# Nine result buffers, stores behind the last load, and the order around them, in a fused recurrence and mixer kernel

## The chip, the cores and the metric

The kernel runs on one core of one Trainium2 chip. The metric is the device time of one execution in microseconds (us). Six engines' queues matter: TensorE (PE, with its weight loads as PEld), VectorE (DVE), ScalarE (ACT), GpSimd (POOL), and SyncE (SP), which issues most DMAs.

## The reference

There are 4 batches of 768 tokens and 8 heads of 40 features. A recurrence with a 40 x 40 state for each batch and head gives `y`; its heads are joined to `x` with 320 features per token, and a mixer follows: a rotation by learned angles, a mix over all 768 tokens of a batch, and a channel product with a residual.

```python
for t in range(S):
    y[:, :, t] = np.einsum('bhd,bhde->bhe', rt, state)
    Sa = np.einsum('bhde,bhe->bhd', state, at)
    state_decay = state * wt[:, :, None, :] - np.einsum('bhd,bhe->bhde', Sa, bt)
    state = state_decay + np.einsum('bhd,bhe->bhde', vt, kt)
...
theta = x @ w_theta
zr, zi = x * np.cos(theta), x * np.sin(theta)
yr = np.einsum('ts,bsd->btd', w_tok_r, zr)
yi = np.einsum('ts,bsd->btd', w_tok_i, zi)
u = x + yr + yi
return u + np.maximum(u @ w_ch, 0.0)
```

Inputs and the result are fp32.

## The kernel before

**Tiles.** The 3072 tokens are cut into 24 tiles of 128 tokens, numbered 0 to 23; tiles 0 to 5 are batch 0, and so on. The recurrence is done chunk by chunk: within a tile by matrix products with triangular masks, from tile to tile by a state (`gt`).

**Operations.** The function builds a list of 1602 operations. An operation has an engine, a kind and a tile, and the text names it by the two: `y20` is the readout of tile 20. A tile goes through these steps:

| kind | engine | what it does | line |
|---|---|---|---|
| `lw lk lb la lv`, `loadr` | SP | loads of the inputs, 160 KB each; `loadr` is issued twice for two tiles | L409, L421 |
| `ln exp ew wi cs cx` | ACT, DVE, PE | decays: logarithm, running sums, exponentials | L445 to L487 |
| `kb ah v r` | POOL mostly | products with the decays, casts to bf16 | L428 to L435 |
| `tkb ta tv tr tb nut xt ut` | PE, or SP | transposes; `ekb` and the like take them out of PSUM (ACT or DVE) | L391, L538, L711; SP: L698 |
| `spsi sphi slv slu` | PE | four sets of scores, 8 matmuls on half the rows each; `mpsi` and the like mask them (DVE; or ACT and then `sel` on POOL) | L569; L578, L580, L582 |
| `x0 nx nu enu` | PE, ACT | solve within the tile; `enu` negates `nu` | L610 to L637 |
| `gt egt wgt gd egd` | PE, DVE, POOL, ACT | the state | L652 to L687 |
| `y ex` | PE, DVE | readout, and the scaling that gives `x` | L785 to L794, L801 |
| `th thj eth sin z` | PE, ACT, POOL, DVE | angles, sines and cosines, products `z`; `thj` is a joint piece of two tiles on half the rows | L755, L765, L820, L842, L857 |
| `row uadd` | PE, DVE | mix over tokens: six chunks of two matmuls for each tile, then `u = x + ...` | L873, L879 |
| `ch chj oo st` | PE, DVE, SP | channel product, `oo` = u + max(., 0) in fp32, and its store | L755, L765, L910, L913 |
| `wdma wt ewt` | POOL, PE, ACT or DVE | load of a block of the token weights (192 KB, real and imaginary part), its transposes | L953, L961, L968 |

The mixing of a batch (`row`) begins when all its tiles have their `z`. So the mixer of one batch runs between the recurrence pieces of the next, and after tile 23 only mixer work is left. Eleven transposes (`CROSSBAR`, L24) are done by DMA from SyncE's queue and not by TensorE: `xt18`, `tkb23`, `ta23`, `nut21`, `tv23`, `ut12`, `tv22`, `nut22`, `xt20`, `ut14`, `ut16`.

**Order.** Nothing is scheduled at run time. `ORDER` (L26) is a written-out permutation of the 1602 operations, each engine issues its own in that order, and semaphores make it wait for what it reads and for buffers to come free. `HOMES` (L122) says which PSUM bank each product gets, in the order of the operations that open one: numbers from 4 on are four single banks, 0 and 2 two double ones. A product waits until the operation that last emptied its bank is done. `PICK` (L138) lists the operations that run on their second engine: for most evacuations ACT and DVE are the two choices, for products POOL and DVE.

**Results and stores.** A result `oo` is written to one of three tiles, `oo_t[t % 3]`, tile 20's to a slot of `th_t`, and stored from SyncE's queue. So `oo` of tile t waits for the store of tile t - 3. Stores 0 to 9 stand between the loads in SyncE's queue, which is in order: a store whose result is not ready holds up the loads behind it.

```python
oo = th_t[0][:, NT - 1] if t == N - 4 else oo_t[t % 3]
ok = ("th", NT - 1) if t == N - 4 else ("oo", t % 3)
...
add("SP", "st", t, lambda bi=bi, j=j, oo=oo: nc.sync.dma_start(
    out=out_r[bi, j], in_=oo), 350, [ok], [], at="row", work=550)
```

The last tile's result is computed and stored in two halves, `oo23` and `oo24`.

Of the kernel before, what the change touches and what calls it, by code (L numbers as in the profile page):

```python
# [9 lines left out]
FP32 = mybir.dt.float32  # L10
BF16 = mybir.dt.bfloat16
AF = mybir.ActivationFunctionType
ALU = mybir.AluOpType
# [197 lines left out]
def kernel(  # L211
# [18 lines left out]
    DM = H * D  # L230
# [819 lines left out]
```

## Time and profile before

| what | value |
|---|---|
| runs | 200.9, 200.0, 199.53 us; median 200.0 |
| the profiled execution | 201.98 us, of which the profiled span is 200.3 us |
| granted TensorE clock over the span | 0.987 |
| busy: TensorE, VectorE, ScalarE, GpSimd | 186.9, 166.5, 150.8, 143.7 us |
| moved by DMA | 32.74 MB, mean 163 GB/s |

The span runs from the first to the last instruction of the program; 1.7 us of the profiled execution lie around it. All places in time below are counted from the start of the span. Matmuls are pipelined and their ends are modelled, so that one's end overlaps the next one's start: two starts tell more than an end and a start. A line belongs to an operation kind; which tile a row belongs to follows from its place in the order.

### The profile page before, as it was taken

Reading aid. Unit: us, or ns where it says so; the run is one execution under the profiler, and the core shown is the slowest. Engines: PE = TensorE matmul, PEld = TensorE weight load, DVE = VectorE, ACT = ScalarE, POOL = GpSimd, SP = SyncE. Lnnn points to the kernel's source line nnn. Section 1 sums busy time; section 2 is a strip of 40 time slices with the busy share of each in tenths; the row PEclk is TensorE's granted clock in tenths of the full one; section 3 lists DMA queues with packets and bytes.
Section 4 is the critical chain, followed back from the end, with each engine's and each line's share of the span. In section 5 each row is a group of like instructions: output and inputs, shape, how many; then the busy total and the mean of one; then the engine's idle time right before and its main releaser. Section 6 shows DMA issues by size and latency. Waiting matters only on the chain.

```text
span 200.3 us, 8005 instructions
## 1 busy us (share of the span) xinstructions
PE 186.9 (93%) x3288; PEld 150.1 (75%) x3288; DVE 166.5 (83%) x265; ACT 150.8 (75%) x334; POOL 143.7 (72%) x208
## 2 busy tenths in 40 slices
PE   6788999996999999997999999999999998899992
PEld 5676787875887788876877878888888767667661
DVE  5369799999899898986787989999999886668653
ACT  4576789899899999698988598889998857476001
POOL 8276556596999999797899947978789894169000
PEclk9799999999999999999999999999999999999998
DMA  6999879999999999999998899899999974625023
GB/s 120 218 181 203 152 159 201 187 175 208 185 176 172 144 219 181 209 185 175 179 225 149 159 213 185 176 164 183 190 198 175 174 103 93 91 69 101 33 98 131
DMA packets 134643, 32.74 MB, mean 163 GB/s; under 512 B 124816, under 2 KB 134608, under 8 KB 134608
## 3 DMA queue, kind: packets, MB, share of 16 engines
q1 hardware_dynamic: 131680, 29.19, 75.2%
q0 software_dynamic: 2784, 2.97, 9.9%
q8 instruction: 25, 0.41, 0.9%
q10 hardware_dynamic: 144, 0.08, 0.1%
q14 instruction: 10, 0.08, 0.1%
HBM read 29.54 MB, written 3.93 MB: 167 GB/s over the span
## 4 chain that ended last, share of the span: by engine, by line
PE 58%; DMA 14%; SPq 8%; POOL 7%; ACT 5%; issue 3%; DVE 3%; DVEq 0%; ACTq 0%; POOLq 0%
PE ps_s L873 13%; PE ps_s L391 8%; PE ps_d L569 7%; PE ps_s L755 5%; SPq L409 5%; SPq L421 3%; DMA raw_r<-in_r_dram 3%; DMA raw_kb<-in_k_dram 2%; DMA raw_a<-in_a_dram 2%; DMA nuT<-nu 2%; PE ps_s L711 2%; PE ps_s L538 2%; DMA xT<-xp 2%; POOL kb L429 2%; PE ps_s L629 2%
## 5 line engine op out<-in xcount | busy, mean ns | idle before, releaser
L429 POOL TENSOR_TENSOR kb<-raw_kb,ex 128x320 bf16<-128x320 f32 x46 | 36.9, 813 | 9.5 <-DMA raw_kb<-in_k_dram 2.7
L873 PE MATMUL ps_s<-zr,wtok_r 128*128 128x320 bf16 x132 | 37.8, 299 | 0.6 <-DVE oo L910 0.4
L873 PE MATMUL ps_s<-zi,wtok_i 128*128 128x320 bf16 x132 | 37.7, 299 | 0.0
L578 DVE TENSOR_TENSOR lamu<-ps_d,mask_p 128x1024 bf16<-128x1024 f32 x23 | 27.9, 1216 | 2.5 <-PE ps_d L569 2.4
L578 DVE TENSOR_TENSOR psi<-ps_d,mask_p 128x1024 bf16<-128x1024 f32 x22 | 26.8, 1216 | 2.0 <-PE ps_d L569 1.8
L578 DVE TENSOR_TENSOR phi<-ps_d,mask_n 128x1024 bf16<-128x1024 f32 x18 | 21.9, 1217 | 1.0 <-PE ps_d L569 1.0
L578 DVE TENSOR_TENSOR lamv<-ps_d,mask_p 128x1024 bf16<-128x1024 f32 x16 | 19.5, 1218 | 2.9 <-PE ps_d L569 2.8
L429 POOL TENSOR_TENSOR ah<-raw_a,we 128x320 bf16<-128x320 f32 x22 | 19.0, 866 | 3.8 <-DMA raw_a<-in_a_dram 2.1
L857 POOL TENSOR_TENSOR zr<-cs,xp 128x320 bf16<-128x320 f32 x21 | 17.3, 828 | 1.7 <-ACT cs L842 1.5
L569 PE MATMUL ps_d<-aT,kbT 64*128 64x128 bf16 x384 | 17.2, 220 | 0.3 <-ACT kbT L394 0.2
L873 PEld LDWEIGHTS <-wtok_r 128*128 128x128 bf16 x144 | 14.0, 97 | 4.5
L873 PEld LDWEIGHTS <-wtok_i 128*128 128x128 bf16 x144 | 14.0, 98 | 4.2 <-issue 0.9
L391 PE MATMUL ps_s<-wide,kb 128*128 128x128 bf16 x184 | 14.8, 223 | 1.7 <-POOL kb L429 1.6
L857 POOL TENSOR_TENSOR zi<-cs,xp 128x320 bf16<-128x320 f32 x18 | 14.1, 795 | 2.7 <-DMA raw_r<-in_r_dram 1.4
L667 POOL TENSOR_TENSOR gt<-sum,ex 128x320 bf16<-128x320 f32 x13 | 9.6, 737 | 8.1 <-DVE sum L663 5.0
L792 PE MATMUL ps_s<-kb,lamv 128*128 128x40 bf16 x192 | 14.8, 180 | 0.0
L794 PE MATMUL ps_s<-kb,lamu 128*128 128x40 bf16 x192 | 14.7, 179 | 0.0
L569 PEld LDWEIGHTS <-kbT 64*128 64x128 bf16 x384 | 12.3, 96 | 2.9 <-ACT kbT L394 1.3
L792 PEld LDWEIGHTS <-lamv 128*128 128x128 bf16 x192 | 13.2, 96 | 0.6
L391 PEld LDWEIGHTS <-kb 128*128 128x128 bf16 x184 | 11.3, 99 | 2.9 <-POOL kb L429 2.3
L469 ACT ACTIVATE ex<-ps_s 128x328 f32<-128x328 f32 (+1 forms) x24 | 10.6, 447 | 3.8 <-PE ps_s L464 1.7
L879 DVE TENSOR_TENSOR up<-ps_s,xp 128x320 bf16<-128x320 f32 x22 | 10.6, 487 | 3.4 <-PE ps_s L873 3.2
(172 smaller groups left out, 602.4 us busy)
## 6 DMA issues: line engine op xcount, KB each, us to landing
raw_w<-in_w_dram SPq DMA_DIRECT2D x24, 160.0 KB, 4.2
raw_v<-in_v_dram SPq DMA_DIRECT2D x24, 160.0 KB, 3.8
raw_a<-in_a_dram SPq DMA_DIRECT2D x24, 160.0 KB, 3.8
raw_kb<-in_k_dram SPq DMA_DIRECT2D x24, 160.0 KB, 4.0
raw_kb<-in_b_dram SPq DMA_DIRECT2D x24, 160.0 KB, 4.3
raw_r<-in_r_dram SPq DMA_DIRECT2D x24, 160.0 KB, 3.8
out_dram<-oo SPq DMA_DIRECT2D x22, 160.0 KB, 2.5
wrow_i<-in_moe_w_tok_i_dram POOLq DMA_DIRECT2D x6, 192.0 KB, 5.1
```

What stands on the lines that cost most here:

```text
L391: nc.tensor.transpose(out=dst[:, c:c + 128], in_=pair(src, g), identity=ident)
L409: lambda dst=dst, src=src: nc.sync.dma_start(out=dst, in_=src),
L429: pool = ("POOL", lambda: nc.gpsimd.tensor_tensor(out=dst, in0=in0, in1=in1, op=ALU.mult))
L469: got = add("ACT", "exp", i, lambda: nc.scalar.activation(out=ex[:, :, 0:D] if no_total else ex.rearrange("p h x -> p (h x)"), in_=sums(ps ...
L569: nc.tensor.matmul(t[:, q, g, :], lhsT=lhs[g][rows(q)], rhs=rhs[g][rows(q)], start=True, stop=True)
L578: add("DVE", kindm, i, lambda: nc.vector.tensor_tensor(out=flat, in0=whole(), in1=mask.to_broadcast([128, 2 * G, 128]), op=ALU.mult), 1217 ...
L755: nc.tensor.matmul(ps(pk)[:, 0:DM], lhsT=lhs[:, 3 * c + kt, :], rhs=wt[:, 3 * c + kt, :], start=kt == 0, stop=kt == 2, skip_group_check=n ...
L792: nc.tensor.matmul(o, lhsT=lamv[:, p, g, :], rhs=kb[:, 0, h, 0:D], start=first, stop=False, skip_group_check=True)
L794: nc.tensor.matmul(o, lhsT=lamu[:, p, g, :], rhs=kb[:, 1, h, 0:D], start=False, stop=True, skip_group_check=True)
L857: pool = ("POOL", lambda: nc.gpsimd.tensor_tensor(out=dst, in0=in0, in1=in1, op=ALU.mult))
L873: nc.tensor.matmul(acc(), lhsT=wtok[nm][j][:, s], rhs=zs[c][:, s], start=n == 0 and c == 0, stop=n == NT - 1 and c == 1)
L879: add("DVE", "uadd", q, lambda: nc.vector.tensor_tensor(out=u, in0=acc(), in1=x, op=ALU.add), 488, [pk, x_key(q)], [u_key(q)], at="row")
```

## The change

1. **Nine result tiles.** A new function `results` gives the result of tile q the home q mod 9: the three `oo` tiles, the two bf16 tiles `o` of the first eight tiles' runs of v, and the four `wrow` tiles into which the token weights were loaded, the last six read as fp32. A result waits for the store nine results earlier, or, the first time, for what last read the borrowed tile. `th_t` is no longer used for it, and the two halves of the last result are tracked apart from their buffer.

```diff
+    def results(q):
+
+        spare = [(("o", n), t.rearrange("p q c d -> p (q c d)")) for n, t in enumerate(o_t)]
+        spare += [(("wrow", nm, n), wrow[nm][n]) for n in range(2) for nm in "ri"]
+        homes = [(("oo", n), t) for n, t in enumerate(oo_t)]
+        homes += [(key, t.bitcast(FP32)[:, 0:DM]) for key, t in spare]
+        return homes[q % len(homes)]
+
...
-                ck, u, oo, ok = ("ps", "ch", q + part), u_of(q), oo_t[q % 3], ("oo", 3 + part)
+                ck, u, (key, oo), ok = ("ps", "ch", q + part), u_of(q), results(q), ("last", part)
...
-                        op0=ALU.max, op1=ALU.add), 320, [ck, u_key(q), ("oo", q % 3)], [ok], at="row")
+                        op0=ALU.max, op1=ALU.add), 320, [ck, u_key(q)] + [key] * part, [ok] + [key] * (1 - part), at="row")
...
-            oo = th_t[0][:, NT - 1] if t == N - 4 else oo_t[t % 3]
-            ok = ("th", NT - 1) if t == N - 4 else ("oo", t % 3)
+            ok, oo = results(t)
```

2. **The lists `ORDER`, `HOMES` and `PICK`.** The set of operations stays the same. Read as names, this is what the new lists change:

- *SyncE.* Stores 3 to 11 leave the stretch of loads. Before: `... lb17 st4 lk17 la17 st3 lv16 ... loadr20 st5 lw22 ... lb21 st7 st6 la21 ... loadr22 st8 st9 xt18 st10 tkb23 ta23 nut21 tv23 st11 ut12 tv22 nut22 xt20 ut14 st13 st12 st15 ut16 st14 st16 st18 st17 st19 ...`. After: `... loadr22 xt18 tkb23 ta23 st3 st4 nut21 tv23 st5 tv22 ut12 nut22 xt20 ut14 st6 st7 st12 st9 st8 ut16 st11 st10 st16 st13 st15 st17 st19 st14 st18 ...`. Loads keep their order among themselves; stores 0 to 2 stay.
- *GpSimd, tiles 6 to 9.* Before: `kb6 wdma2 wdma2 kb7 ah7 kb7 r6 z2 wdma3 z2 z2 z2 wdma3 kb8 kb8`. After: `kb6 wdma2 ah7 wdma2 kb7 wdma3 kb7 wdma3 r6 kb8 z2 z2 z2 kb8`. `wdma2` loads block 0 of the token weights, `wdma3` block 1.
- *TensorE, tiles 5 to 9.* Before: `x05 cs8 tb6 tkb6 nu5 ta6 tb7 gd4 nut5 spsi6 sphi6 ta7 tkb7 slu5 x06 tr6 spsi7 nu6 y4 y5 gt6`. After: `x05 tb6 cs8 ta6 nu5 tkb6 y4 nut5 spsi6 gd4 sphi6 tb7 tkb7 ta7 slu5 x06 tr6 spsi7 nu6 y5 nut6 gt6`, and other changes up to `row0`. From there to `row9` TensorE's order is the same.
- *TensorE, from row9 on.* The order is new up to the end. Around the places that the text speaks of, before: `y20 row12 row12 row14 gd20 ... x021 row13 row12 slv21 sphi22 nu21 row13 row14 row12 gt21 row12 row14 row14 row12 row13 sphi23 spsi22 th18 th19 row13 gd21 thj18 slu21` and `y21 row15 gt22 ... nu23 row16 row16 row16 nut23 th21 th20`. After: `y20 row12 row12 row14 row14 row12 row13 x021 row13 row14 row13 nu21 sphi22 slv21 row12 row12 gt21 row14 row14 row14 row12 row13 spsi22 sphi23 gd21 th19 row13 row13 th18 x022 thj18 slu21` and `y21 row15 row15 gt22 row15 row15 ch13 ch12 chj12 slv22 slv23 x023 row16 row16 gd22 row16 row16 nu23 slu22 row16 row16 nut23 th20 th21`.
- *Engines.* Fifteen evacuations, masks and casts (three of the masks with their second step on GpSimd) and eleven products `z` change engine. After it VectorE has 236 of the operations (240 before), ScalarE 327 (324), GpSimd 185 (183).
- *Homes.* `row12` now takes the bank that `ekb22` empties; before, it took the one that `oo11` empties.

216 rows, old and new, of tables (HOMES, ORDER, PICK) are left out of this document.

## The prediction

> **What bounds the kernel now.** I read the page first (engines, then the chain that ended last), then the table of stretches, then the timeline of TensorE with what released it, and last SyncE's and GpSimd's side of those places.
>
> ```profile
> span 200.3 us, 8005 instructions
> PE 186.9 (93%) x3288; PEld 150.1 (75%) x3288; DVE 166.5 (83%) x265; ACT 150.8 (75%) x334; POOL 143.7 (72%) x208
> ...
> PE 58%; DMA 14%; SPq 8%; POOL 7%; ACT 5%; issue 3%; DVE 3%; DVEq 0%; ACTq 0%; POOLq 0%
> ```
>
> TensorE is busy for 93% of the span and makes up most of the last chain. The table by stretch (length, busy time of each engine, granted clock, DMA share, GB/s) says where the other 7% lie:
>
> ```profile
> 40.00:50.20 10.20, 8.54 (x161) 6.72 (x158) 10.11 (x14) 9.89 (x22) 7.97 (x12) 1.00 1.05 192
> 50.20:88.00 37.80, 37.52 (x749) 31.04 (x750) 34.87 (x47) 33.95 (x79) 35.53 (x51) 1.00 1.06 183
> 88.00:96.00 8.00, 6.89 (x133) 5.85 (x132) 5.56 (x10) 6.84 (x15) 6.53 (x9) 1.00 1.01 183
> 96.00:142.00 46.00, 45.72 (x847) 37.81 (x843) 41.52 (x63) 39.24 (x87) 37.05 (x51) 1.00 0.94 183
> 142.00:157.00 15.00, 14.99 (x306) 12.47 (x304) 14.06 (x23) 13.45 (x31) 13.68 (x19) 1.00 1.01 193
> 157.00:177.00 20.00, 18.08 (x276) 13.26 (x275) 14.28 (x24) 11.69 (x20) 12.22 (x15) 1.00 0.62 108
> 177.00:196.70 19.70, 19.37 (x189) 13.39 (x188) 14.73 (x27) 7.16 (x16) 6.52 (x8) 1.00 0.25 65
> ```
>
> From 50.2 to 157 TensorE idles 0.3, 1.1, 0.3 and 0.0 us per stretch: it runs its order without holes, so only less work on it or fewer holes make the kernel shorter. Holes within reach of the change are at 40 to 50 (1.7 us) and at 157 to 177 (1.9 us). Four waits make up most of them (start, length, what ended the idle time before):
>
> ```profile
> 50.24 0.62 PE L538 MATMUL ps_s<-wide,r 128*128 128x128 bf16 x8 [1.10 <-POOL r L435]
> ...
> 51.34 0.20 PE L785 MATMUL ps_s<-gd,rT 128*128 128x80 bf16 x1
> 51.88 0.20 PE L785 MATMUL ps_s<-gd,rT 128*128 128x80 bf16 x1
> ```
>
> ```profile
> 156.31 0.21 PE L785 MATMUL ps_s<-gd,rT 128*128 128x80 bf16 x1
> ...
> 157.47 0.30 PE L873 MATMUL ps_s<-zr,wtok_r 128*128 128x320 bf16 x1 [0.44 <-DVE oo L910]
> ```
>
> ```profile
> 165.90 0.31 PE L765 MATMUL ps_s<-wth,xT 64*128 64x320 bf16 x2
> 166.74 0.41 PE L569 MATMUL ps_d<-rT,nuT 64*128 64x128 bf16 x8 [0.52 <-DMA nuT<-nu]
> ```
>
> ```profile
> 174.33 0.39 PE L391 MATMUL ps_s<-wide,nu 128*128 128x128 bf16 x4
> 175.56 0.72 PE L755 MATMUL ps_s<-wth,xT 128*128 128x320 bf16 x4 [0.84 <-DMA xT<-xp]
> 176.21 0.31 PE L765 MATMUL ps_s<-wth,xT 64*128 64x320 bf16 x2
> 176.35 0.34 PE L569 MATMUL ps_d<-rT,nuT 64*128 64x128 bf16 x6
> ```
>
> These rows, four short cuts of TensorE's timeline, hold tr6 (50.24), row12 (157.47), slu21 (166.74) and th21 (175.56). Modelled ends overlap, so I take a hole from starts. A readout y lasts 0.54 (51.34 to 51.88); y20 began at 156.31, so row12 could have begun at 156.85 and lost **0.62**. A thj piece takes 0.14 (176.21 to 176.35), so slu21 lost 166.74 - 166.04 = **0.70**. Four transposes take 0.23 (47.12 to 47.35, quoted below), so th21 lost 175.56 - 174.56 = **1.00**.
>
> **The change, part by part.** *Nine result buffers.* Where before a result waited for the store of the third result before it, it now waits for the ninth. VectorE shows one such wait, and it is what row12 waits for, since oo11 empties the bank that row12 fills:
>
> ```profile
> 156.92 0.89 DVE L910 SCALAR_TENSOR_TENSOR oo<-ps_s,up 128x320 f32<-128x320 f32 x2 [0.67 <-DMA out_dram<-oo]
> ```
>
> ```profile
> 153.58 3.22 DMA out_dram<-oo
> ```
>
> The second row is from the chain: the store issued at 153.58 took 3.22 us to land. In the new order row12 fills the bank that ekb22 empties, row14 that of oo10, and none of oo3 to oo22 waits for a store younger than nine results. I count -0.62. The first use of the borrowed tiles waits for work of tiles 4 and 6 and for weights long since transposed: nothing.
>
> *Stores 3 to 11 behind the last load.* This takes nine issues out of SyncE's queue among the loads and lets the loads move up. On TensorE that is worth nothing: where most of these stores stood, 96 to 157, it idles 0.3 of 61 us. The cover is TensorE's own full queue; were that gone, the gain would be the time of the nine issues. They move to 157 to 185, where the DMA share is 0.62 and then 0.25, but there they stand beside the transposes through DMA that slu21 and th21 wait for:
>
> ```profile
> 161.49 0.44 ACT nu L633
> 161.96 4.73 DMA nuT<-nu
> ...
> 169.95 0.49 DVE xp L801
> 171.07 4.44 DMA xT<-xp
> ```
>
> SyncE's new order there is tkb23, ta23, st3, st4, nut21, tv23, st5, tv22, ut12, nut22, xt20, ut14. The two stores ahead of nut21 fill time in which SyncE waited for nu21's result anyway; xt20 has none right ahead of it.
>
> *New order around slu21 and th21.* Between nu21 and slu21 the new order has nine chunks of mixing product, four sets of scores, gt21, gd21, x022, th18, th19 and thj18, 88 matmuls where there were 60. With 0.27 for a chunk (two of the 14 matmuls in the next row), 0.24 for a set of scores and 0.08 for each change between whole and half arrays (below) I estimate 5.4 us from the start of nu21. The transpose is issued 0.85 after that start (0.4 of matmuls, 0.44 for the negation at 161.49) and lands after 4.73 as before: 5.6. slu21's hole shrinks to 0.2.
>
> ```profile
> 184.75 1.90 PE ps_s L873 x14
> ```
>
> For th21 the same sum goes from y21. Twenty-two pieces, 6.2 us, now lie before th20, which has taken th21's place in front. Against them stand the readout (0.7), eth19 and ex21 on VectorE (0.6 beyond it) and the landing (4.44): 5.7. The 1.00 goes. So the two waits give -0.50 and -1.00.
>
> *y4 ahead of tr6.* tr6 is held by the cast r6, and this by a load that lands at 49.4; none of SyncE's order ahead of it changes. y4 stood after tr6 and now stands before it, where TensorE waits: -0.54. It needs what y5 needs, of one tile earlier.
>
> *The token-weight loads.* GpSimd's wait for r6's data, its group of token-weight issues, and their landing:
>
> ```profile
> 49.47 0.72 POOL L435 CAST r<-raw_r 128x640 bf16<-128x640 f32 x1 [1.69 <-DMA raw_r<-in_r_dram]
> ```
>
> ```profile
> L953 POOL DMA_DIRECT2D wrow_i<-in_moe_w_tok_i_dram x6 | 3.5, 592 | 0.0
> ```
>
> ```profile
> wrow_i<-in_moe_w_tok_i_dram POOLq DMA_DIRECT2D x6, 192.0 KB, 5.1
> ```
>
> The two issues of 0.59 each move from behind r6 into the 1.69 before it, and one of block 0 moves behind ah7. GpSimd gains 1.2 us from 50.2 on, but TensorE idles only 0.3 of the 37.8 us after it: worth 0. Their data, 2 x 192 KB at 192 GB/s, are 2.0 us of a DMA share that is already full (1.05). Bounds: 0 if they arrive behind r6's data, +2.0 if ahead. I take 0: issued at 47 and 48.5 and landing some 5 us later, they come behind data that land at 49.4.
>
> *Changes of array shape.* Scores and the joint pieces use half the rows. Counted over the two orders, TensorE changes between whole and half 126 times before and 134 times after.
>
> ```profile
> 46.25 0.38 PE L391 MATMUL ps_s<-wide,nu 128*128 128x128 bf16 x4
> 46.56 0.62 PE L569 MATMUL ps_d<-aT,kbT 64*128 64x128 bf16 x16
> 47.12 0.40 PE L391 MATMUL ps_s<-wide,ah 128*128 128x128 bf16 x4
> 47.35 0.88 PE L391 MATMUL ps_s<-wide,kb 128*128 128x128 bf16 x8
> ```
>
> Four transposes take 0.23 before another whole-array piece (47.12 to 47.35) and 0.31 before scores (46.25 to 46.56): 0.08 a change. Two of the eight lie before tr6, inside its wait; six cost **+0.48**.
> The Trainium skill ("TensorEngine Tiling (Array Packing)", Key Properties) says that changing the tiling mode drains the TensorE. The trace agrees in kind. By a whole drain, estimated as the 0.15 by which the modelled 0.38 of such a piece outlasts its 0.23, six changes would cost 0.9 and the sum below would be 0.4 higher.
>
> *Moves between engines.* Some thirty evacuations, products and masks change engine or place: VectorE loses four operations, ScalarE gains three, GpSimd two. The middle is untouched. From 142 to 157 TensorE has no hole at all, so the new order there can only add some: y17, gt19 and slu18 move nearer to what they wait for. Nearest rows, in a dense stretch: holes of 0 to 0.7 each. I allow +0.6 net for all of these, less 0.4 for holes under 0.25 at 162 to 164 that the order dissolves: **+0.2**, with bounds -0.4 and +2.3 (all that was won comes back).
>
> *The end.* oo23, the last tile's first half, now waits for st14, which stands behind st19. At 1.8 us a landing it comes about when oo23 is due: 0 to 0.4, taken as 0.
>
> **The sum.** -0.62 - 0.50 - 1.00 - 0.54 + 0.48 + 0.2 = **-2.0**. The profiled execution took 201.98 with its span of 200.3; the median of the runs is 200.0. The difference is set against the median: 198.0. Because I took nut21's and xt20's landings at their slow value, and faster ones are as likely, I place the forecast at **197.8 us**, own range 196.8 to 199.2.
>
> **Rivals.** *The waits come back* (no change). The order was taken apart at the only places where TensorE waited; the new one has other neighbours, each ready within 0.1 or 0.2. If the three holes of 157 to 177 reappear in other places at their old size of 2.3, -0.54 + 0.48 is left: 199.9. For it: two of the three were landings, which no order shortens. Against it: the cover grew by 0.4 us and more for each.
>
> *Stores ahead of transposes* (slower). SyncE's queue and its DMA ring are one line. If nut21 lands one store later, 4.73 + 3.22 = 8.0 against a cover of 4.6, slu21 waits 3.4; then ut12, behind st5, makes ch13 wait by up to 3.2 less 0.6 of slack. 198.0 + 3.2 (the wait beyond the 0.2 counted) = 201.2 with the first alone, 203.8 with both; I put it at 202.5. It decides once both together cost over 4 us. For it: landings of 4.73 at a DMA share of only 0.62. Against it: both stores can be issued while SyncE waits for the negation, and the DMA share leaves room for them.
> The Trainium skill ("DMA: Bandwidth & Descriptors", Queues, rings and completion order) states that on each DMA engine descriptors are consumed in ring order. By that rule a transpose does stand behind such a store; the trace before has no store issued right ahead of nut21 to price it.
>
> *The change does little of what it says.* The buffers remove one wait of 0.62 and the store moves nothing; if the orders alone decide, nothing of it is left but the 0.62: 199.4. It falls to the cases within 1%.
>
> **Chances.** Forecast 0.55, of which 0.40 lie below 198.0; waits back, or only the buffers, 0.25; stores ahead of transposes 0.20. So faster by over 1% (2.0 us, about what a measurement of this kernel tells from no change) 0.40, within 1% 0.40, slower by over 1% 0.20. The range for 8 in 10 runs from 196.4 (no new hole, all landings fast) to 202.4, which takes in the waits that come back and half of the slower case.
>
> **What would show it.** Right: tr6 still begins near 50.2 with y4 before it; row12 follows y20 without idle; the waits for nuT and xT in 157 to 177 fall from 1.4 to under 0.4 us; the row of 157 to 177 has under 0.8 idle; the last matmul ends about 2 us earlier. Wrong: TensorE idle for over 0.5 us in 142 to 157, a landing of nuT over 6 us, tr6 after 51, or a wait for uT.

## The result and the profile after

The kernel after takes **198.31 us** (median of 6 runs, 197.24 to 200.83) against 200.76 for the kernel before (6 runs beside it, 199.53 to 202.49). The ratio is 0.9874, 95% interval 0.9833 to 0.9915: 1.7 to 3.4 us less. Ratios here leave out runs over 1.5% above the fastest of the same kernel. A second comparison (e11 below) gave 0.9892, interval 0.9845 to 0.9939. The profiled execution of the kernel after took 199.53 with a span of 197.8. The forecast was 197.8, a drop of 2.2 from the 200.0 of the three runs then known; it was met. Faster by over 1% had been given 0.40, as much as within 1%; the middle of the interval lies there, its lower end (0.85%) doesn't. The sum behind the forecast was right only in part.

The page of the profile after: span; share of the span and instructions of each engine; and the chain that ended last.

```profile
span 197.8 us, 8019 instructions
PE 187.6 (95%) x3288; PEld 150.3 (76%) x3288; DVE 164.3 (83%) x261; ACT 151.7 (77%) x337; POOL 145.1 (73%) x210
...
PE 68%; DMA 9%; ACT 8%; SPq 6%; DVE 3%; issue 3%; POOL 1%; ACTq 0%; DVEq 0%; POOLq 0%
```

DMA's part of the chain fell from 14% to 9% and GpSimd's from 7% to 1%; TensorE's rose from 58% to 68%. The table by stretch of the kernel after (length, then busy time of TensorE, weight loads, VectorE, ScalarE, GpSimd; granted clock, DMA share, GB/s) stands against the one in the prediction:

```profile
40.00:50.20 10.20, 9.78 (x193) 7.73 (x190) 10.18 (x14) 9.81 (x23) 8.76 (x14) 1.00 0.99 180
50.20:88.00 37.80, 36.60 (x724) 30.34 (x723) 34.72 (x45) 33.53 (x80) 34.01 (x49) 1.00 1.08 189
88.00:96.00 8.00, 7.91 (x148) 6.48 (x146) 6.50 (x12) 7.87 (x16) 8.00 (x11) 1.00 1.04 187
...
142.00:157.00 15.00, 15.00 (x306) 12.25 (x304) 14.74 (x23) 13.83 (x34) 13.36 (x18) 1.00 0.72 129
157.00:177.00 20.00, 20.00 (x320) 14.95 (x317) 15.70 (x25) 14.69 (x24) 14.22 (x17) 1.00 0.70 146
```

From 157 to 177 TensorE's idle time went from 1.92 to 0.00. From 40 to 50.2 it fell from 1.66 to 0.42, but from 50.2 to 88 it rose from 0.28 to 1.20, and from 88 to 96 it fell from 1.11 to 0.09. So the later of the two new orders gave a clean gain, and the earlier one moved its holes about. TensorE's timeline after, at tr6 (50.91), row12 (157.20), slu21 (165.51) and the theta products of tiles 20 and 21 (173.62):

```profile
50.21 0.35 PE L616 MATMUL ps_s<-v,psi 128*128 128x40 bf16 x8
50.91 0.62 PE L538 MATMUL ps_s<-wide,r 128*128 128x128 bf16 x8 [0.35 <-POOL r L435]
...
156.65 0.21 PE L793 MATMUL ps_s<-gd,rT 128*128 128x80 bf16 x1
157.20 0.30 PE L881 MATMUL ps_s<-zr,wtok_r 128*128 128x320 bf16 x1
...
165.36 0.31 PE L773 MATMUL ps_s<-wth,xT 64*128 64x320 bf16 x2
165.51 0.39 PE L569 MATMUL ps_d<-rT,nuT 64*128 64x128 bf16 x8
...
173.34 0.39 PE L391 MATMUL ps_s<-wide,nu 128*128 128x128 bf16 x4
173.62 0.72 PE L763 MATMUL ps_s<-wth,xT 128*128 128x320 bf16 x4
```

row12 follows the start of y20 by 0.55, which is what a y takes; slu21 and th20 follow their neighbours by 0.15 and 0.28. tr6 still waits, with y4 already done. The new hole stands behind it. This is the chain of waits of the kernel after from 48 to 56 (start, length, what):

```profile
48.11 6.82 DMA raw_w<-in_w_dram
54.93 0.02 issue
54.95 0.03 ACT lw L445
54.98 0.35 issue
55.33 0.36 ACT nuT L394
55.69 0.04 issue
55.73 0.44 PE ps_s L711 x5
```

Tile 9's decay load lw9 takes 6.82 to land (4.92 in the trace before). ScalarE stands in ln9 (L445) until then; nut6's evacuation (L394) is queued behind it, and xt4 (L711) needs that bank. xt4 begins 0.9 late.

### The profile page after: what moved, and what is told of

The parts are those of the page before. It is cut to its first block, busy times and chain, and to the rows that moved or that the text cites. A ratio compares the mean times of both kernels' runs of the same rounds, so it can differ in the third digit from the quotient of the medians.

```text
span 197.8 us, 8019 instructions
## 1 busy us (share of the span) xinstructions
PE 187.6 (95%) x3288; PEld 150.3 (76%) x3288; DVE 164.3 (83%) x261; ACT 151.7 (77%) x337; POOL 145.1 (73%) x210
## 4 chain that ended last, share of the span: by engine, by line
PE 68%; DMA 9%; ACT 8%; SPq 6%; DVE 3%; issue 3%; POOL 1%; ACTq 0%; DVEq 0%; POOLq 0%
PE ps_s L881 17%; PE ps_s L391 10%; PE ps_d L569 9%; PE ps_s L763 5%; SPq L409 4%; DMA raw_w<-in_w_dram 3%; DMA raw_kb<-in_k_dram 3%; PE ps_s L711 3%; PE ps_s L652 2%; PE ps_s L629 2%; SPq L421 2%; DMA raw_r<-in_r_dram 2%; PE ps_s L538 2%; PE ps_s L773 2%; ACT cs L850 2%
## 5 line engine op out<-in xcount | busy, mean ns | idle before, releaser
L881 PE MATMUL ps_s<-zr,wtok_r 128*128 128x320 bf16 x132 | 37.6, 299 | 0.0
L578 DVE TENSOR_TENSOR lamu<-ps_d,mask_p 128x1024 bf16<-128x1024 f32 x22 | 26.8, 1219 | 1.7 <-PE ps_d L569 1.6
L578 DVE TENSOR_TENSOR lamv<-ps_d,mask_p 128x1024 bf16<-128x1024 f32 x17 | 20.7, 1218 | 2.6 <-PE ps_d L569 1.8
L578 DVE TENSOR_TENSOR phi<-ps_d,mask_n 128x1024 bf16<-128x1024 f32 x17 | 20.7, 1218 | 0.9 <-PE ps_d L569 0.8
L865 POOL TENSOR_TENSOR zi<-cs,xp 128x320 bf16<-128x320 f32 x21 | 16.9, 816 | 3.3 <-ACT cs L850 3.3
L865 POOL TENSOR_TENSOR zr<-cs,xp 128x320 bf16<-128x320 f32 x19 | 15.3, 810 | 0.7 <-ACT cs L850 0.7
L569 PEld LDWEIGHTS <-kbT 64*128 64x128 bf16 x384 | 11.8, 94 | 3.1 <-ACT kbT L394 1.0
L435 POOL CAST r<-raw_r 128x640 bf16<-128x640 f32 x12 | 8.6, 720 | 6.5 <-DMA raw_r<-in_r_dram 6.5
L445 ACT ACTIVATE lw<-raw_w 128x320 bf16<-128x320 f32 x24 | 11.4, 475 | 2.6 <-DMA raw_w<-in_w_dram 2.6
```

The source lines that it names most:

```text
L445: add("ACT", "ln", i, lambda: nc.scalar.activation(out=paired(lw)[:, :, :, 0:D], in_=paired(raw_w[s4]), func=AF.Ln), 473, [("raw_w", s4)], ...
L569: nc.tensor.matmul(t[:, q, g, :], lhsT=lhs[g][rows(q)], rhs=rhs[g][rows(q)], start=True, stop=True)
L578: add("DVE", kindm, i, lambda: nc.vector.tensor_tensor(out=flat, in0=whole(), in1=mask.to_broadcast([128, 2 * G, 128]), op=ALU.mult), 1217 ...
L865: pool = ("POOL", lambda: nc.gpsimd.tensor_tensor(out=dst, in0=in0, in1=in1, op=ALU.mult))
L881: nc.tensor.matmul(acc(), lhsT=wtok[nm][j][:, s], rhs=zs[c][:, s], start=n == 0 and c == 0, stop=n == NT - 1 and c == 1)
```

## The experiments

Two marks make the traces comparable, since tb5, before the first change, begins anywhere from 36.1 to 38.6: the stage from thj2 (the joint theta piece of tiles 2 and 3) to nu10, which holds the first new order, and the stage from th15 to ch22, the last product, which holds the second. Lengths from the starts of these pieces in each trace:

| kernel | order in tiles 5 to 9 | thj2 to nu10 | order from row9 on | th15 to ch22 |
|---|---|---|---|---|
| before | before | 36.91 | before | 58.63 |
| e3 | before | 36.28 | before | 57.78 |
| e12 | before | 38.34 | before | 57.06 |
| e1 | after | 37.60 | before | 57.90 |
| e2, e10 | before | 35.98, 38.27 | after | 56.27, 56.27 |
| after, e11 | after | 37.11, 36.28 | after | 56.05, 55.95 |
| e4, e5, e6 | after | 36.87, 37.43, 36.31 | after | 55.94, 55.95, 56.06 |

In e10's earlier stage the granted clock was 0.96, in all others of the table 1.00. So the clock doesn't explain the differences of the later stage; the 0.987 over the span before comes from its first 20 us (0.91) and its last 10 (0.92). (e7, e8 and e9 change these stages and are told on their own.)

**e1, the first window alone.** The two orders agree on the set of operations among their first 702 places, so they can be cut and joined there.

```diff
-ORDER, HOMES, PICK = before
+ORDER = after[:702] + before[702:]   # HOMES, PICK per operation likewise
```

> The kernel before with only the first of the two new orders, tiles 5 to 9 (with the token-weight loads put earlier); three result buffers, the stores and the order near slu21 and th21 as before. Theory (from the trace after): a wash. y4 fills tr6's wait, but the token weights now stand ahead of tile 9's loads, ScalarE waits for them in ln9 and TensorE loses 0.85 at xt4; what is left is settled again by the wait at tkb13 (94.7 in both traces). So 200.7, ratio to before 1.000 (0.997 to 1.003), a hole of about 0.9 near 55 and one of under 0.4 at tkb13. Rival, the prediction's terms: y4 -0.54 and two switches inside the wait, 200.1, ratio 0.997, no hole after tr6.

Measured: 202.22, ratio 1.0092 (1.0040 to 1.0143). The first window alone gains nothing and by this run rather costs. The trace doesn't show where: its tb5, ahead of the first change, began 1.9 later than before, with a granted clock of 0.93 from 20 to 45. The hole at xt4 was only 0.25 here, but slu7 and ta8 waited 0.5 and 0.8 for ScalarE's nuT and GpSimd's ah8.

**e2 and e10, the second window alone.**

```diff
-ORDER, HOMES, PICK = after
+ORDER = before[:702] + after[702:]   # nine buffers and stores as after
```

> The kernel after with the order, the banks and the token-weight loads of before in tiles 5 to 9; nine buffers, stores behind the last load and the new order near slu21 and th21 as in the kernel after. Theory: all of the gain is here: 198.3, ratio to before 0.988 (0.985 to 0.991), tkb13 waits 1.2 again and 157 to 177 has no hole. Rival, the prediction's terms: this window gives -0.62 - 0.50 - 1.00 + 0.48 + 0.2 = -1.4, ratio 0.993.

> The kernel of e2 once more (order of before in tiles 5 to 9, all else as after), on one chip beside the kernel after, to settle the sign of the first window. By the traces the stage from thj2 to nu10 takes 36.4 in the order of before (three traces: 36.91, 35.98, 36.28) and 37.1 in that of after (37.11, 37.61, 36.87, 36.31 with its loads early). Theory: the first window costs 0.3 to 1.0, so this kernel is faster than after by that. Rival, the prediction's: the first window gains 0.1 to 0.5, so this kernel is slower than after by that.

> The kernel after, unchanged, beside the two others on one chip: ratio to before 0.987 to 0.990, the stage from thj2 to nu10 near 37.1, no hole over 0.1 on TensorE in 157 to 177, row12 without a wait for VectorE.

Measured: e2 198.43, ratio 0.9899 (0.9848 to 0.9951); e10 198.34, 0.9862 (0.9803 to 0.9921); beside it the kernel after as e11, 198.73, 0.9892 (0.9845 to 0.9939). The second window alone gives the whole gain; its later stage is 0.3 longer than with both, by a wait within x022. What the first does stays open: e1 says a cost of 0.4 to 1.4%, e10 against e11 none that can be told, and its stage takes 36.0 to 38.3 with the old order and 36.3 to 37.6 with the new. My theory of a standing cost of 0.3 to 1.0, read from single traces, isn't shown; the prediction's small gain isn't either. The two stages, as rows of the table by stretch (e1 the later stage with the old order, e11 with the new; then the earlier stage of e2, old, and e11, new):

```profile
139.36:197.26 57.90, 56.25 (x844) 42.49 (x842) 46.78 (x76) 36.66 (x74) 34.79 (x44) 1.00 0.59 117
...
136.21:192.16 55.95, 55.66 (x845) 42.27 (x843) 44.06 (x72) 37.72 (x76) 36.30 (x46) 1.00 0.56 123
...
43.58:79.56 35.98, 34.87 (x711) 28.95 (x710) 34.51 (x47) 34.12 (x79) 34.44 (x50) 1.00 1.07 189
...
43.28:79.56 36.28, 35.40 (x711) 28.94 (x710) 34.64 (x46) 34.30 (x80) 34.47 (x50) 1.00 1.08 195
```

**e3, the buffers alone.**

```diff
-            oo = th_t[0][:, NT - 1] if t == N - 4 else oo_t[t % 3]
+            ok, oo = results(t)          # all orders as before
```

> The kernel before with its own orders and stores, but nine result buffers in place of three. Theory of the prediction: row12's 0.6 at 157.5 goes and nothing else changes: 200.1, ratio 0.997 (0.994 to 1.000). Rival: the 0.6 comes back at slu21, whose landing of nuT stays (1.3 there instead of 0.7), and the kernel is as before, 1.000. A third reading, that the buffers are what lets the whole second window close up, would give 198.3.

Measured: 200.95, ratio 1.0027 (0.9975 to 1.0078). No gain. The waits of TensorE from 140 to 180 (engine, what it did, what it waited for: us in total, times, longest), first before, then e1, which has three buffers too:

```profile
PE ps_s L755 <- DMA xT<-xp: 0.8, 1, 0.8
PE ps_d L569 <- DMA nuT<-nu: 0.5, 1, 0.5
PE ps_s L873 <- DVE oo L910: 0.4, 1, 0.4
```

```profile
PE ps_s L754 <- DMA xT<-xp: 0.9, 1, 0.9
PE ps_d L568 <- DMA nuT<-nu: 0.4, 1, 0.4
```

e1 has no wait of row12 for VectorE, although its results still share three buffers, and neither has the trace of e12, so the third row belongs to one execution, in which a store took 3.22 us. The two waits for transposes stand. Whether the new order from row9 on would gain as much with three buffers, no run tells.

**e4, stores among the loads.**

```diff
 SP: ... lb17, +st4, lk17, la17, +st3, ... loadr20, +st5, lw22, ... lb21, +st7, +st6, la21, ...
-SP: ta23, st3, st4, nut21, tv23, st5, ... ut14, st6, st7, st12
+SP: ta23, nut21, tv23, ... ut14, st12
```

> The kernel after with five of the nine moved stores, st3 to st7, put back among the loads where the kernel before has them; all else as after. Theory of the prediction: the stores' place is worth nothing: 198.3, ratio to before 0.988, and TensorE has no hole from 142 to 157. Rival: the loads of tiles 21 to 23 land up to 2.6 us later and the new order, made for the earlier ones, waits for one of them: 1.0 more, 199.3, ratio 0.993, with a hole of about 1 between 142 and 152.

Measured: 198.39, ratio 0.9924 (0.9871 to 0.9976); TensorE has no hole from 142 to 157 and the later stage takes 55.94, as with the stores moved. The place of these stores is worth nothing that shows. They are all that the change took from among the loads: in SyncE's order before, st8 to st11 already stood behind the last load.

```profile
142.00:157.00 15.00, 15.00 (x283) 12.23 (x280) 14.74 (x22) 13.81 (x32) 13.46 (x20) 1.00 0.73 144
```

**e5, the token-weight loads back.**

```diff
-POOL: wdma2, ah7, wdma2, kb7, wdma3, kb7, wdma3, r6, kb8, z2, z2, z2
+POOL: wdma2, wdma2, ah7, kb7, kb7, r6, kb8, wdma3, z2, z2, z2, wdma3
```

> The kernel after with only GpSimd's token-weight loads put back where the kernel before issues them (two behind r6, one ahead of ah7). Theory: in the kernel after these two transfers of 192 KB stand ahead of tile 9's loads, lw9 lands 6.8 to 8.1 after its issue instead of 4.9 to 6.2, ln9 holds ScalarE, and TensorE loses 0.9 at xt4 (in the runs after and e4). Put back, lw9 lands within 6.2, the hole at xt4 is under 0.3, the stage from thj2 to nu10 takes 36.4 instead of 37.1, and the kernel 197.6, ratio to before 0.984. Rival (the prediction's 0 for these loads): the transfers are limited by the full DMA share in either order, the hole of 0.9 stays or moves, 198.3, ratio 0.988.

Measured: 199.55, ratio 0.9939 (0.9887 to 0.9990). Half right: lw9 landed in 6.29 and xt4 had no hole. But the time was not won: ta8 now waited for GpSimd's ah8. Among the waits of TensorE in e5 (us in total, times, longest):

```profile
PE ps_s L390 <- POOL ah L428: 2.4, 2, 1.3
```

The stage took 37.43, no less than with the loads early. The traces of e6 and e11, with the loads early, have no hole at xt4 either; over 0.2 it is in four of the six traces with them early (after, e1, e4, e7) and in none of the six with them late (before, e2, e3, e5, e10, e12). So the loads are its likely cause, and one trace doesn't show it. The hole goes from piece to piece in a stage whose DMA share is full (1.07 in e5).

**e6, ten more changes of array shape.**

```diff
-chj4 sphi14 spsi14 row6    x014 ut6 slv14 sphi16    tv15 thj12 spsi15    chj6 slv15 spsi16 row8 row8
+chj4 sphi14 row6 spsi14    x014 slv14 ut6 sphi16    thj12 tv15 spsi15    chj6 row8 slv15 row8 spsi16
```

> The kernel after with five of TensorE's pieces moved by one place between tkb14 and gd14, where it has no wait, so that it changes between whole and half arrays 144 times instead of 134; the same matmuls. This stage took 14.58 in all six traces so far. By the prediction's price of 0.08 a change: 15.4. By a whole drain of 0.15 a change: 16.1. If a change costs nothing: 14.6. Up to 0.2 may come on top from two pieces that are ready just late.

Measured: 199.56, ratio 0.9956 (0.9904 to 1.0009). The stage from tkb14 to gd14, after and e6:

```profile
107.39:121.97 14.58, 14.56 (x256) 11.88 (x254) 12.60 (x20) 11.46 (x27) 11.37 (x15) 1.00 0.95 170
...
105.30:121.05 15.75, 15.71 (x256) 11.71 (x254) 12.91 (x20) 11.44 (x27) 12.15 (x16) 1.00 0.97 174
```

1.17 us for ten changes, of which up to 0.1 or 0.2 are two pieces ready just late: **0.10 to 0.12 a change**. The prediction's 0.08 was low. The Trainium skill ("TensorEngine Tiling (Array Packing)", Key Properties) says that a change of tiling mode drains TensorE; the 0.15 that I had estimated for a whole drain is too much by the same rows.

**e7, four more stores ahead of transposes.**

```diff
-SP: ... st3, st4, nut21, ... nut22, xt20, ut14, st6, st7, st12, st9, st8, ...
+SP: ... st3, st4, st6, st7, nut21, ... nut22, st8, st9, xt20, ut14, st12, ...
```

> The kernel after with four more of the moved stores put right ahead of transposes on SyncE's queue: st6 and st7 ahead of nut21 (behind st3 and st4), st8 and st9 ahead of xt20. The prediction's slower rival: a transpose lands one store's landing later for each, so nut21 and xt20 take over 6 from issue to landing, slu21 and th21 wait 2 and more each, 201.5 or over, ratio 1.00. Theory: only the issues cost, 0.5 each, nut21 and xt20 go out 1.0 later and land in the same 2.4 to 4.5; holes of 0.3 at slu21 and 0.9 at th21: 199.5, ratio 0.993.

Measured: 201.40, ratio 1.0021 (0.9980 to 1.0063), some 1.3% above the kernel after. The profiled execution took 203.68, its later stage 57.83 at a granted clock of 1.00. slu21, in the timeline, and its cause, in the chain:

```profile
169.43 0.34 PE L568 MATMUL ps_d<-rT,nuT 64*128 64x128 bf16 x6 [1.52 <-DMA nuT<-nu]
```

```profile
164.72 4.66 DMA nuT<-nu
```

So with two further stores ahead of nut21 the gain is lost, but not as the slower rival had it. nut21 took 4.66, not over 6, and no more than the 4.4 to 4.8 of the old order with no store right ahead; xt20, with two stores ahead, took 3.45 with no wait of th21. What the stores cost is the time of issue, about 0.5 for each further one: nut21 went out 2.50 after the start of nu21, against 1.1 to 1.3 with two stores ahead (after, e2, e5, e6, e10, e11) and 0.87 with none (before, e1, e3, e4, e12). 2.50 + 4.66 is over the 5.5 of work between nu21 and slu21; with a landing of 2.4 it would not have been. The Trainium skill ("DMA: Bandwidth & Descriptors", Queues, rings and completion order) has descriptors consumed in ring order on each DMA engine; no run here shows a transpose held up by that.

**e8 and e9, other orders.** These two kernels take the order that a model of the engines, fed with the durations and landings of the traces, found best.

```diff
 # e8: TensorE, ScalarE, VectorE, GpSimd reordered by steps of up to six places
 # e9: TensorE, VectorE, GpSimd only; ScalarE as after
-ORDER = after
+ORDER = <the model's best>
```

> A version of the kernel after with the order of TensorE, ScalarE, VectorE and GpSimd planned once more over the whole kernel, by moves of up to six places, against the landings of the loads in all six traces so far instead of one (130 changes of array shape; SyncE's queue, the buffers and the engine of each operation as after). Theory: the holes that depend on a run's load landings (tr6, xt4, slu7, ta8, tkb13) are covered better: 1 to 1.8 less than after, 196.5 to 197.3, ratio to before 0.980. Rival: what the loads set cannot be reordered away and other landings open other holes: 198.3, ratio 0.988.

> As e8, but ScalarE keeps the order of the kernel after (e8 had 343 instructions there instead of 337: six more table loads of 1.28, since sines and exponentials were mixed); only TensorE, VectorE and GpSimd are ordered anew, against the load landings of eight traces, at 0.105 for a change of array shape (128 changes instead of 134). Theory: six fewer changes give 0.6 and holes that depend on landings give up to 1: 1 to 1.5 less than the kernel after, ratio to before 0.981 to 0.984. Rival: the holes move as in e5 and only the changes of shape count: ratio 0.986.

Measured: e8 214.86, ratio 1.0696 (1.0639 to 1.0754); e9 202.17, ratio 1.0046 (1.0016 to 1.0076). Neither theory held; both are slower than the kernel after. Two groups of ScalarE, e8 and then after:

```profile
L849 ACT ACT_TABLE_LOAD x8 | 10.3, 1283 | 0.1
L1023 ACT ACT_TABLE_LOAD x7 | 9.0, 1283 | 0.1
```

```profile
L850 ACT ACT_TABLE_LOAD x5 | 6.4, 1283 | 0.1
L1024 ACT ACT_TABLE_LOAD x4 | 5.1, 1283 | 0.1
```

e8 has six table loads more, 7.7 us of ScalarE, that its theory had not counted; its granted clock was also lower, 0.94 to 0.97 from 40 us on, and how the loss divides between the two stays open. For e9, with none more, single waits are named in the trace (0.8 of cs14 for ScalarE's gd, 0.8 of tv9 for VectorE's sum), and its later stage took 58.13, but not why an order expected to be 1 to 1.5 us better than the kernel after came out about 3 worse. That stays open.

**e12, the code transfers.** Nothing explained yet why the same transpose lands in 2.4 or in 4.7.

```diff
-WARM = {21: 25, 30: 4, 33: 1, 28: 8, 41: 11}
+WARM = {21: 17, 30: 2, 33: 1, 28: 5, 41: 7}
```

> The kernel before with 17 of its 49 warm-up matmuls at the start left out (they work on a constant and their sums are thrown away), all else as before. In the trace before, two of the 25 transfers of 16 KB on the instruction queue begin at 164.47 and 173.31, while nut21 (issued 161.96) and xt20 (171.07) are in flight; over the eleven traces so far each transpose with such a transfer in its first 2.5 lands in 3.4 to 4.7, the others in 2.4 to 2.7. They come at fixed places of TensorE's instruction stream, every 256 instructions; 34 instructions fewer ahead of them put them at about 166 and 175. Theory: nut21 and xt20 then land in about 2.5, slu21 and th21 wait for nothing, and the stage from th15 to ch22 takes 56.3 instead of 57.8: ratio to before 0.992, with no reordering at all. Rival: the long landings belong to the transposes or to the other traffic there: landings of 4.4 to 4.7, stage 57.8, ratio 1.000, or slower by what the missing warm-ups cost at the start (up to 0.5).

Measured: 200.62, ratio 0.9978 (0.9934 to 1.0021). The edit did not move the transfers as meant: they began at 164.41 and 173.37, beside the same pieces as before. But xt20, issued at 171.01, landed in 2.60, when the second of them had only just begun (2.36 after the issue, 2.24 in the trace before); th21 waited for nothing, and the later stage took 57.06. nut21 landed in 4.76 and slu21 waited as ever. DMA queues and issues in the first 2.3 us of xt20, before and then e12 (queue, kind: packets, MB, share of time; transfer, median us to landing):

```profile
q8 instruction: 1, 0.02, 2.9%
issues: line engine op xcount, KB each, median us to landing
xT<-xp SPq DMA_TRANSPOSE x1, 4.4
```

```profile
q1 hardware_dynamic: 1162, 0.28, 60.3%
issues: line engine op xcount, KB each, median us to landing
xT<-xp SPq DMA_TRANSPOSE x1, 2.6
```

## Why the prediction was right, and where not

By its terms, against what stands in several traces:

- **row12, -0.62: wrong.** The step that failed is "I count -0.62" from one late store, set against the median of the runs. e1 and e12 have no such wait with three buffers, e3 gains nothing with nine.
- **slu21 and th21, -0.50 and -1.00: right.** Both waits stand with the old order (e1: 0.4 and 0.9 by the releasers; th21 not in e12) and are under 0.1 in all traces with the new one save e7 (e9 has an order of its own). The reason given, more cover between issue and use, is shown for th21: xT still lands in 4.3 to 4.4 after and in e11, and th20 in front waits under 0.1. For slu21 it is only half the reason. The cover came out as forecast, 5.52 from nu21 to slu21 (5.4 estimated). But the two stores ahead of nut21 do not fit into time in which SyncE waited anyway, as was argued: in the trace after, nut21 went out 1.28 after nu21's start at 159.99, not 0.85. SyncE's issues there, the two stores and then nut21 (start, length, what):

```profile
160.13 1.05 SPq L920 DMA_DIRECT2D out_dram<-o  x2
161.27 1.20 SPq L698 DMA_TRANSPOSE nuT<-nu  x1
```

  With the forecast landing of 4.73 slu21 would still have waited 0.5. It did not because nuT landed in 4.08 after, and in 2.4 in e2, e4, e5, e6, e10 and e11. The prediction had called faster landings as likely as slow ones, without a reason; this much was luck.
- **Moves between engines, +0.2: wrong in sign.** The small holes of 0.2 each in the chunks of row12 and row14 went, as counted (-0.4), and the +0.6 of new ones did not come: 142 to 177 has none.
- **y4 ahead of tr6, -0.54: came, and was given back.** tr6 waits 0.4 to 1.4 in the traces with the old order and 0.1 to 0.5 with the new. Behind it there are holes at xt4, slu7 or ta8, in some traces as large; the stage's length shows no gain.
- **Token-weight loads, 0 with a bound of +2.0: the bound bit.** "They come behind data that land at 49.4" is the step that failed: after, lw9 took 6.82 to land and TensorE lost 0.9 at xt4. That the loads did it is likely (e5 above), not shown; that putting them back wins the stage's length is refuted.
- **Changes of shape, +0.48: price too low.** At 0.11 the eight are 0.9. Two, 0.2, lie in the later stage; six lie in tiles 5 to 9, where 0.6 or so can't be told from the stage's scatter of 2 and stand against what y4 gained.
- **Stores, 0, and the tail, 0: right** (e4; from ch22 to the end of the span 4.2 before, 4.1 after). But five issues left the stretch of loads, not nine.

The later stage closes: -0.5 - 1.0 - 0.4 + 0.2 = -1.7, against 57.8 (e1, e3) to 56.0 (after, e4, e5, e11), -1.8; the 58.6 before holds row12's 0.6 as well. The sum of -2.0 met the measured 1.7 to 3.4 because 1.2 of gain that did not last (row12, y4) stood against 0.9 of cost that did not show in the length (moves 0.6, changes of shape 0.3). That these nearly cancel is luck; the terms for slu21, th21 and the small holes are what the result rests on. Of the rivals, the waits did not come back where it counts, and two stores ahead of nut21 delayed it by 0.2 to 0.4 without a wait. Of the third, the stores' place is worth nothing, as it said (e4); but the buffers alone don't give its 0.62 (e3), and the order from row9 on, with the nine buffers, gives the whole gain.

## What to carry to other kernels

A wait seen in one profiled execution is a term of the sum only if its cause stands in every execution: a dependence that was late in all traces of the old order (nuT), or in all but one (xT), was worth its size, a store that landed late once (row12), or a load whose lateness changes from run to run (tr6), was not. In the stage here whose DMA share was full, filling one hole moved it; where the loads had ended, cover between issue and use stayed won. Compare stages between fixed pieces, not spans: here that showed 0.1 us where whole runs scatter by 2.

## What was not expected of the hardware

- **Code transfers and transposes.** The page of the profile counts 25 transfers of 16 KB on an instruction queue. Of fourteen traces, xt20 landed in 3.4 to 4.5 in the twelve where one began 0.6 to 2.25 us after its issue, and in 2.6 in the two where it began at 2.36 or later (e12, e4). nut21 landed in 2.4 where it began at 2.2 or later, in 4.1 to 4.7 where earlier (after, e8, e7), and also in 4.4 to 4.8 where an 8 KB transfer of a second instruction queue began 1.8 to 1.9 after its issue (before, e1, e3, e12). The other transposes agree on the 16 KB: xt18 landed in 4.1 to 4.4 where one began 1.15 to 1.21 after its issue (before, e3, e12) and in 2.7 in the nine traces where none began between 0.05 after it and the landing; nut22, with none before it landed, in 2.4 to 2.5 in all fourteen. On the 8 KB they don't: ta23 landed in 2.4 to 2.7 in eight traces where one began 0.8 to 0.9 after its issue, as in the others. The 2.5 of e12's expectation was too wide. The Trainium skill ("Runtime: NRT & Kernel Launch", Instruction fetch mechanics) gives blocks of 16 KiB or 256 instructions and calls their cost mostly hidden; the size agrees, the transposes in flight took up to 2 us longer. That the transfers cause it is argued from their times alone: e12 was to move them and did not, and why is open.
- **A stall without a cause in the trace.** nu16's evacuation begins 0.27 later in every trace with the new order of tiles 5 to 9, though its inputs are as early; the stage from gd14 to tv18 takes 10.88 instead of 10.60. No run here shows why.
